# r of two batches by one transfer each, unused tables out, and new order tables, in an RWKV attention and MLP-mixer kernel

## The chip, the cores and the metric

The kernel runs on one core of a Trainium2 chip. A core has five instruction queues that run side by side: TensorE (PE, matrix products, with its weight loads shown apart as PEld), VectorE (DVE), ScalarE (ACT), GpSimd (POOL) and SyncE (SP, which here only issues transfers). Transfers run on 16 DMA engines; those that SP issues go through a hardware queue (q1 in the profile), those that POOL issues through a software queue (q0), which can convert f32 to bf16 on the way. The metric is the device time of one execution in microseconds (us), lower is better. A profile is taken of one execution and records when each instruction and each DMA packet ran.

## What is computed

The reference has two parts. The first is a linear attention with decay for 4 batches, 8 heads, 768 steps and a head size of 48:

```python
for t in range(S):
    kt, vt, rt = (k[:, :, t], v[:, :, t], r[:, :, t])
    cur = np.einsum('bhd,bhe->bhde', u[None] * kt, vt)
    y[:, :, t] = np.einsum('bhd,bhde->bhe', rt, state + cur)
    state = w[None, :, :, None] * state + np.einsum('bhd,bhe->bhde', kt, vt)
```

Its result, turned to x of 768 steps by 384 columns a batch, goes through an MLP mixer:

```python
xt = x.transpose(0, 2, 1)
h = np.maximum(xt @ w_tok1, 0.0) @ w_tok2
u = x + h.transpose(0, 2, 1)
h2 = np.maximum(u @ w_ch1, 0.0) @ w_ch2
return (u + h2).astype(np.float32)
```

w_tok1 is 768 by 256, w_tok2 256 by 768, w_ch1 384 by 1536 and w_ch2 1536 by 384. All inputs and the output are f32.

## The kernel before

**Chunks.** The 768 steps of a batch are 6 chunks of 128 steps. In a chunk the recurrence becomes matrix products: k and r are multiplied by tables of powers of the decay w (`wnat` for k; `wp`, or `wpair`, for r), rounded to bf16 (`kr`), and turned so that the head dimension lies on the partitions (`trk`, `tr_ps`, copied to `rka`, `rkb`). The scores (`at_ps`) are their products, a mask makes `AT` of them, and `y_ps` sums AT times v and r times the state `S` of the chunk before. The state itself (`kv_ps`) grows by k times v. The step's own term with u is a small sum (`pr`, `ad_ps`, `adg`) times v (`own`, written to `ydb` or `yd`). The sum goes to `x_b` in bf16.

**The loads.** k and v come per chunk: a tile of 128 partitions (steps) with 8 runs of 48 floats, 192 bytes each, 192 KB. For batches 0 and 1 (`wide`), r comes per window of two chunks: a partition holds two steps, the runs are 384 bytes, and a load `win` is 384 KB (lines 506 to 538); three buffers `win` take turns. For batches 2 and 3, r comes per chunk (`rt`). SP issues all of these. `HOLD` makes a load wait until another has landed, so about three loads of batch 0 are under way at a time; `GATES` makes a load wait for a weight.

**The weights.** POOL issues seven weight transfers, `w0` to `w6` (lines 540 to 563): w_tok1, w_tok2, the first third of w_ch1 (columns 0 to 511), the rest of w_ch1, and three parts of w_ch2. `W_DEP` says which load of k or v must have landed before each goes out. POOL is in order, so a weight also waits for the products that stand ahead of it there.

**The mixer.** For each batch: `hid` (x_b by w_tok1 into `h1_ps`, 12 products of 384 columns in one to three parts), `relu` into `h1r`, `back` (by w_tok2; for batch 0 added to turned x_b, `turn_x`, into `hx_ps` and copied to `uT`), 24 tasks `up` of 3 products (`z_ps`, by w_ch1), 24 `relu` into `zr`, and `down` (`h_ps`, by w_ch2), then `osb` and a store. Products `up` with index 0 to 3 need only w2, the others w3.

**The order.** The kernel does not run its loops as written. Each piece of work is a task with dependencies (`add`, `flex`); `Plan.run` (line 245) emits all of them in the order of the list `ORDER`, written out at the top. `ENGINES` says which of two engines does a task that either could do, `BUFS` which buffer of a pool each tile takes. Each engine then runs its instructions in just this order, and each waits for its semaphores. So `ORDER`, `BUFS`, `ENGINES`, `W_DEP`, `HOLD` and `GATES` set all queues. All instructions that the tasks emit carry one line, 294, of a helper, so the profile's groups are told apart by their tiles.

Around the change the queues of before stand like this (chunk numbers of batch 0 unless said; k0 is k of chunk 0). SP: r of window 0, r of window 1, k0, k1, r of window 2, v1, k3, k2, k4, v0, v2, v3, v4, k5, v5, then for batch 1: r of window 0, k0, v0, r of window 1, k2, v1, v2, k1, r of window 2. POOL, after tables and products: w0, `own` of chunks 0 and 2, a product of k5, w1, `own` of 3 and 4, w2, w3, and then products of batch 1. w0 waits for v2, w1 and w2 for k5, w3 for v3.

At the start PE runs 12 products of zeros (`NWARM`, `warm`), and `FILL` puts a few more in front of single tasks. `pairs` (lines 654 to 798), the table `wnpair`, `mask2`, `place` and some pools belong to a way of working on two chunks at a time that is switched off (`PAIRED = []`); the tables are still built.

Of the kernel before, what the change touches and what calls it, by code (L numbers as in the profile page):

```python
# [67 lines left out]
    0, 1, 2, 0, 1, 0, 2, 1, 0, 2, 1, 0, 2, 1, 0, 1, 2, 0, 1, 2, 0, 1, 2, 0,  # L68
],
    'AT1': [  # L70
    0, 1, 2, 0, 1, 0, 2, 1, 0, 2, 1, 0, 2, 0, 1, 2, 0, 1, 2, 0, 1, 2, 0, 1,
# [11 lines left out]
    0, 1, 2, 3, 4, 1, 0, 2, 3, 4, 1, 0, 2, 3, 1, 4, 0, 2, 3, 4, 1, 0, 2, 3,  # L83
],
    'adg2': [],
# [4 lines left out]
    0, 1, 2, 3, 4, 5, 0, 1, 4, 2, 3, 0, 4, 5, 1, 2, 3, 0, 5, 4, 1, 2, 3, 0, 5, 2, 1, 0, 3, 4,  # L90
],
    'krw': [],
    'kt': [
    0, 1, 2, 3, 4, 5, 0, 1, 2, 3, 4, 5, 0, 1, 2, 3, 4, 5, 0, 1, 2, 3, 5, 4,
],
    'ku': [
    0, 1, 2, 0, 0, 0, 2, 0, 1, 2, 1, 2,
# [13 lines left out]
],  # L111
    'osb': [
    0, 1, 2, 0, 1, 2, 2, 2, 1, 0, 0, 1, 2, 0, 1, 2, 0, 1, 2, 0, 1, 2, 0, 1, 2,
],
    'pr': [
    0, 1, 1, 0, 1, 0, 1, 0, 1, 0, 1, 1,
],
    'pr2': [],
    'rk': [
    0, 1, 2, 3, 0, 1, 3, 2, 0, 1, 2, 3,  # L120
],
    'rka': [
    0, 1, 2, 0, 1, 2, 0, 1, 2, 0, 1, 2,
],
    'rka2': [],
# [4 lines left out]
    0, 1, 0, 1, 0, 1, 0, 1, 0, 1, 0, 1,  # L130
# [4 lines left out]
    'rwin': [],  # L135
    'uT': [
    0, 1, 2, 3, 1, 0, 3, 2,
],
    'u_sb': [
    0, 1, 2, 0, 1,  # L140
],
    'vb': [
    0, 1, 2, 3, 4, 0, 1, 3, 2, 4, 0, 1, 2, 3, 0, 3, 4, 1, 3, 1, 2, 0, 4, 3,
],
    'vb2': [],
    'vt': [
    0, 1, 2, 3, 4, 5, 0, 1, 3, 2, 4, 5, 0, 1, 3, 2, 4, 5, 0, 1, 3, 2, 4, 5,
],
    'win': [
    0, 1, 2, 1, 0, 2,  # L150
],
    'yd': [
    0, 1, 2, 0, 1, 2, 0, 1, 2, 0, 1, 0, 2, 1, 0, 1, 2, 0,
],
    'ydb': [
    0, 1, 0, 1, 0, 1,
],
    'zr': [
    0, 1, 2, 1, 0, 1, 2, 0,
# [1065 lines left out]
```

## Time and profile before

| What | us |
|---|---|
| three runs | 165.94, 165.34, 166.04 |
| their median | 165.94 |
| span of the profiled execution, first to last instruction | 160.1 |
| PE busy | 153.4 |
| PE weight loads (beside PE) | 102.6 |
| DVE busy | 111.6 |
| POOL busy | 88.8 |
| ACT busy | 68.2 |

The time of the profiled execution as a whole is not listed beside its span; the median of the runs is 5.8 us above the span. In the lines of a timeline the columns are start in us, duration in us, engine, line, operation, tiles written and read with their shapes, count, and in brackets the idle time of the engine just before with what ended it. "SPq" and "POOLq" are the sequencers that issue transfers. PE's matmuls are pipelined, so the mean duration of one is longer than the distance between two.

### The profile page before, as it was taken

To read this page: it belongs to the slowest core of one execution; us is meant where nothing else is said; L and a number is where in the kernel's file an instruction comes from. 1 tells how busy PE (TensorE), PEld (TensorE's weight loads), DVE (VectorE), ACT (ScalarE), POOL (GpSimd) and SP (SyncE) were. 2 spreads that over 40 slices of the span, in tenths; PEclk is the share of its full clock that TensorE was granted. 3 is DMA by queue.
4 is the path that set the end of the run, shared out by engine and by line. 5 is a ranking of instruction groups with operands and counts; after the bars stand their busy time and mean duration, and the time that the engine had idled before them with its cause. 6 is when DMAs were issued, how large, how long until landed. Compare 5 with 4: busy or idle time off the path is not lost.

```text
span 160.1 us, 3797 instructions
## 1 busy us (share of the span) xinstructions
PE 153.4 (96%) x1463; PEld 102.6 (64%) x1463; DVE 111.6 (70%) x237; ACT 68.2 (43%) x150; POOL 88.8 (55%) x112
## 2 busy tenths in 40 slices
PE   6998799899999999999999999999999999999992
PEld 1464577567677677666767666677676556676572
DVE  6689884875697578397969939788997357422432
ACT  3999875438924254254524431144214102355000
POOL 7149991028179999899982997999822000000000
DMA  5999999999999979999999999999791064300222
GB/s 130 208 208 182 147 236 220 207 230 212 186 203 204 196 164 186 220 215 150 246 205 207 213 211 161 197 232 205 120 265 57 0 158 161 74 6 0 98 98 98
DMA packets 93061, 26.89 MB, mean 168 GB/s; under 512 B 87794, under 2 KB 92148, under 8 KB 93044
## 3 DMA queue, kind: packets, MB, share of 16 engines
q1 hardware_dynamic: 90688, 23.40, 72.6%
q0 software_dynamic: 2160, 3.15, 11.5%
q8 instruction: 11, 0.18, 0.5%
q10 hardware_dynamic: 196, 0.11, 0.2%
q14 instruction: 6, 0.05, 0.1%
HBM read 20.46 MB, written 4.72 MB: 157 GB/s over the span
## 4 chain that ended last, share of the span: by engine, by line
PE 76%; DMA 17%; ACT 2%; POOL 1%; issue 1%; SPq 1%; DVE 0%; POOLq 0%
PE h_ps L294 34%; PE z_ps L294 27%; DMA wch<-in_moe_w_ch_dram 7%; DMA kt<-in_k_dram 5%; DMA vt<-in_v_dram 5%; PE y_ps L294 4%; PE at_ps L294 3%; PE hT_ps L294 3%; PE kv_ps L294 2%; PE hx_ps L294 1%; PE trk L294 1%; ACT vb L294 1%; SPq L294 1%; PE tr_ps L294 1%; ACT x_b L294 1%
## 5 line engine op out<-in xcount | busy, mean ns | idle before, releaser
L294 PE MATMUL h_ps<-wch,zr 128*128 128x384 bf16 (+1 forms) x300 | 53.9, 320 | 0.0
L294 PE MATMUL z_ps<-uT,wch 128*128 128x384 bf16 x288 | 52.5, 327 | 0.6 <-DMA wch<-in_moe_w_ch_dram 0.6
L294 ACT ACTIVATE zr<-z_ps 128x384 bf16<-128x384 f32 x56 | 27.1, 492 | 39.5 <-PE z_ps L294 39.3
L294 PEld LDWEIGHTS <-wch 128*128 128x128 bf16 x288 | 31.1, 115 | 13.4 <-DMA wch<-in_moe_w_ch_dram 1.2
L294 PEld LDWEIGHTS <-zr 128*128 128x128 bf16 x300 | 27.6, 98 | 15.3
L294 DVE TENSOR_TENSOR AT<-at_ps,mask 128x512 bf16<-128x512 f32 x48 | 31.0, 683 | 3.7 <-PE at_ps L294 3.6
L294 DVE TENSOR_SCALAR zr<-z_ps 128x384 bf16<-128x384 f32 x40 | 21.4, 554 | 11.4 <-PE z_ps L294 8.6
L294 POOL TENSOR_TENSOR yd<-vb,adg 128x384 f32<-128x384 bf16 x18 | 14.8, 828 | 11.6 <-ACT vb L294 4.3
L294 POOL TENSOR_TENSOR kr<-kt,wnat 128x384 bf16<-128x384 f32 x19 | 19.3, 1019 | 3.0 <-DMA kt<-in_k_dram 2.9
L294 ACT CAST vb<-vt 128x384 bf16<-128x384 f32 x22 | 11.0, 511 | 12.6 <-DMA vt<-in_v_dram 12.6
L294 DVE TENSOR_TENSOR osb<-u_sb,h_ps 128x384 f32<-128x384 bf16 (+1 forms) x16 | 8.4, 528 | 9.9 <-PE h_ps L294 9.4
L294 PEld LDWEIGHTS <-kr 128*128 128x128 bf16 x176 | 11.8, 102 | 4.9 <-POOL kr L294 1.5
L294 POOL TENSOR_TENSOR ku<-kt,u_bc 128x384 f32<-128x384 f32 x12 | 12.1, 1008 | 0.5 <-DMA kt<-in_k_dram 0.5
L294 POOL TENSOR_TENSOR rku<-ku,rt 128x384 f32<-128x384 f32 x12 | 11.9, 1001 | 0.2
L294 POOL TENSOR_TENSOR kr<-rt,wp 128x384 bf16<-128x384 f32 x12 | 12.0, 1000 | 0.0
L294 PEld LDWEIGHTS <-wtok 128*128 128x128 bf16 x78 | 7.4, 98 | 4.4
L294 DVE TENSOR_TENSOR x_b<-y_ps,yd 128x384 bf16<-128x384 f32 x18 | 9.6, 549 | 0.6 <-PE y_ps L294 0.5
L294 PE MATMUL h_ps<-x_b,wtok 128*128 128x384 bf16 x48 | 8.8, 327 | 0.0
L294 PE MATMUL y_ps<-vb,AT 128*128 128x48 bf16 x192 | 8.7, 184 | 0.0
L294 ACT CAST S<-kv_ps 48x192 bf16<-48x192 f32 x18 | 5.6, 311 | 7.3 <-PE kv_ps L294 4.2
L294 POOL TENSOR_TENSOR pr<-rka,rkb 128x512 bf16<-128x512 bf16 x2 | 2.3, 1149 | 10.7 <-DVE rka L294 10.7
L294 DVE TENSOR_TENSOR u_sb<-x_b,hT_ps 128x384 bf16<-128x384 bf16 x15 | 7.6, 548 | 0.6 <-PE hT_ps L294 0.6
(93 smaller groups left out, 183.1 us busy)
## 6 DMA issues: line engine op xcount, KB each, us to landing
kt<-in_k_dram SPq DMA_DIRECT2D x24, 192.0 KB, 4.2
vt<-in_v_dram SPq DMA_DIRECT2D x24, 192.0 KB, 4.8
out_dram<-osb SPq DMA_DIRECT2D x23, 192.0 KB, 1.9
win<-in_r_dram SPq DMA_DIRECT2D x6, 384.0 KB, 4.9
rt<-in_r_dram SPq DMA_DIRECT2D x12, 192.0 KB, 3.2
wch<-in_moe_w_ch_dram POOLq DMA_DIRECT2D x4, 384.0 KB, 6.6
wtok<-in_moe_w_tok_dram POOLq DMA_DIRECT2D x2, 384.0 KB, 6.4
wch<-in_moe_w_ch_dram POOLq DMA_DIRECT2D x1, 768.0 KB, 11.3
```

Source lines behind the costliest of these rows:

```text
L294: return lambda *args, **kw: tc.keep_in_program_order(f(*args, **kw))
```

## The change

The diff, cut to its core; the lists `ORDER`, `BUFS` and `ENGINES` are replaced as a whole.

```diff
-W_DEP = [(0, 2, 2), (0, 5, 0), (0, 5, 0), (0, 3, 2), (1, 2, 0), (1, 1, 2), (1, 5, 0)]
-HOLD = {(0, 4, 1): (0, 2, 1),
...
-GATES = {(2, 0, 2): 1, (2, 4, 1): 3, (3, 1, 0): 2, (3, 1, 1): 6, (3, 5, 2): 5}
-NWARM = 12
...
-FILL = {138: 2, 154: 1, 159: 1, 190: 1}
+W_DEP = [(0, 0, 2), (0, 4, 2), (0, 5, 2), (0, 5, 2), (1, 1, 0), (1, 2, 0), (1, 1, 2)]
+HOLD = {(0, 2, 0): (0, 1, 0),
+        (0, 0, 2): (0, 0, 0),
+        (0, 1, 2): (0, 3, 0),
+        (0, 2, 2): (0, 2, 0),
+        (0, 4, 0): (0, 0, 2),
+        (0, 5, 0): (0, 1, 2),
+        (0, 3, 2): (0, 2, 2),
+        (0, 4, 2): (0, 4, 0),
+        (0, 5, 2): (0, 5, 0),
+        (1, 0, 1): (0, 3, 2),
+        (1, 0, 0): (0, 4, 2)}
+GATES = {(1, 0, 0): 2}
+NWARM = 17
...
+FILL = {130: 3, 171: 1, 185: 2}
...
-    t_wn2 = [decay(wn2, j, j, [t_io2]) for j in range(2)]
...
     def load(b, c, i):
         nm, src = (("kt", k), ("rt", r), ("vt", v))[i]
-        win = two_steps(b, c, i)
-        nm = "win" if win else nm
+        whole = i == 1 and wide(b)
 
         def f():
-            if win:
-                t = sb("win", [128, H, 2 * D], f32)
-                dst = t
-                what = src[b, :, ds(c * T, 2 * T), :].rearrange("h (p j) d -> p h (j d)", j=2)
+            if whole:
+                t = sb("rw", [128, H * NWIN, 2 * D], f32)
+                got = sp.dma_start(t, src[b].rearrange("h (w p j) d -> p (h w) (j d)", p=T, j=2))
+                for cc in range(C):
+                    asked[b, cc, i] = got
+                    loaded[b, cc, i] = t.rearrange("p (h w) e -> p h w e", w=NWIN)[:, :, cc // 2, :]
             else:
...
```

A key is (batch, chunk, input), with input 0 for k, 1 for r and 2 for v. One buffer `rw` of 1152 KB takes the place of the three `win`; the r of batch 1 goes into the same buffer, so it waits until all r products of batch 0 have read it. `mask2`, `place`, `wnpair` and `pairs` go. The Exp tables that only batches 2 and 3 use (`wnat` for groups of three chunks, `wp`) and their state tables are mostly built later.

The built program of the changed kernel has these queues. SP: r of batch 0, k1, k0, k3, k2, v0, v1, v2, k4, k5, v3, v4, v5, then r of batch 1, k0, k1, k2, k3, v0, v1, k5, k4 of batch 1. POOL: products of r and k, the u product, the mask, w0, a `pr`, a table, `own` of 0 and 1, a product of k4, `own` of 2, a `pr`, `own` of 3, w1, w2, w3, then two products of batch 1's r. `own` of chunks 4 and 5 is on DVE. On DVE, the two products of r for window 1 of batch 1 stand after the copy of the last x_b of batch 0 and ahead of the second `relu` into `h1r`; on PE their turn stands ahead of the first `back`, and the turn of window 0 ahead of the first `up`. Of the tasks that either engine could do, 64 `relu` into `zr` and `h1r` are on ACT and 40 on DVE (60 and 44 before).

More of the change, by code (lines that the diff above doesn't have):

```diff
@@ L67 @@
     'AT0': [
-    0, 1, 2, 0, 1, 0, 2, 1, 0, 2, 1, 0, 2, 1, 0, 1, 2, 0, 1, 2, 0, 1, 2, 0,
+    0, 1, 2, 1, 0, 2, 1, 0, 2, 1, 0, 2, 0, 1, 2, 0, 1, 0, 2, 0, 1, 2, 0, 1,
 ],
     'AT1': [
-    0, 1, 2, 0, 1, 0, 2, 1, 0, 2, 1, 0, 2, 0, 1, 2, 0, 1, 2, 0, 1, 2, 0, 1,
+    0, 1, 2, 1, 0, 2, 1, 0, 2, 1, 0, 2, 0, 1, 2, 1, 0, 2, 1, 2, 0, 1, 2, 0,
 ],
@@ L82 @@
     'adg': [
-    0, 1, 2, 3, 4, 1, 0, 2, 3, 4, 1, 0, 2, 3, 1, 4, 0, 2, 3, 4, 1, 0, 2, 3,
+    0, 1, 2, 3, 4, 0, 1, 2, 3, 4, 0, 2, 1, 4, 0, 3, 2, 4, 1, 0, 4, 3, 2, 0,
 ],
-    'adg2': [],
     'h1r': [
@@ L89 @@
     'kp': [
-    0, 1, 2, 3, 4, 5, 0, 1, 4, 2, 3, 0, 4, 5, 1, 2, 3, 0, 5, 4, 1, 2, 3, 0, 5, 2, 1, 0, 3, 4,
+    0, 1, 2, 3, 4, 5, 0, 2, 1, 4, 3, 2, 0, 5, 1, 4, 2, 0, 5, 3, 4, 2, 1, 0, 5, 3, 2, 4, 0, 1,
 ],
-    'krw': [],
     'kt': [
-    0, 1, 2, 3, 4, 5, 0, 1, 2, 3, 4, 5, 0, 1, 2, 3, 4, 5, 0, 1, 2, 3, 5, 4,
+    0, 1, 2, 3, 4, 5, 0, 1, 2, 3, 5, 4, 0, 1, 3, 2, 5, 4, 0, 1, 3, 2, 5, 4,
 ],
     'ku': [
-    0, 1, 2, 0, 0, 0, 2, 0, 1, 2, 1, 2,
+    0, 1, 2, 0, 1, 2, 0, 1, 2, 0, 1, 0,
 ],
@@ L102 @@
     'm': [
[8 rows of a table removed]
[7 rows of a table added]
 ],
     'osb': [
-    0, 1, 2, 0, 1, 2, 2, 2, 1, 0, 0, 1, 2, 0, 1, 2, 0, 1, 2, 0, 1, 2, 0, 1, 2,
+    0, 1, 2, 0, 1, 0, 0, 2, 2, 2, 0, 0, 0, 2, 2, 0, 1, 2, 2, 1, 2, 0, 1, 2, 0,
 ],
     'pr': [
-    0, 1, 1, 0, 1, 0, 1, 0, 1, 0, 1, 1,
+    0, 1, 0, 1, 0, 1, 1, 0, 1, 0, 1, 0,
 ],
-    'pr2': [],
     'rk': [
-    0, 1, 2, 3, 0, 1, 3, 2, 0, 1, 2, 3,
+    0, 1, 2, 3, 0, 1, 2, 3, 1, 0, 2, 3,
 ],
     'rka': [
-    0, 1, 2, 0, 1, 2, 0, 1, 2, 0, 1, 2,
+    0, 1, 2, 0, 1, 2, 0, 2, 1, 0, 2, 0,
 ],
-    'rka2': [],
     'rkb': [
@@ L129 @@
     'rku': [
-    0, 1, 0, 1, 0, 1, 0, 1, 0, 1, 0, 1,
+    0, 1, 1, 0, 1, 0, 1, 0, 0, 1, 0, 1,
 ],
@@ L134 @@
 ],
-    'rwin': [],
+    'rw': [
+    0, 0,
+],
     'uT': [
@@ L139 @@
     'u_sb': [
-    0, 1, 2, 0, 1,
+    0, 1, 2, 0, 2,
 ],
     'vb': [
-    0, 1, 2, 3, 4, 0, 1, 3, 2, 4, 0, 1, 2, 3, 0, 3, 4, 1, 3, 1, 2, 0, 4, 3,
+    0, 1, 2, 3, 4, 0, 1, 2, 3, 4, 0, 2, 1, 3, 0, 1, 4, 3, 0, 2, 1, 3, 4, 2,
 ],
-    'vb2': [],
     'vt': [
[L147 to L150, printed above, removed]
+    0, 1, 2, 3, 4, 5, 0, 1, 2, 3, 4, 5, 0, 1, 3, 4, 0, 2, 1, 5, 3, 4, 0, 2,
 ],
     'yd': [
-    0, 1, 2, 0, 1, 2, 0, 1, 2, 0, 1, 0, 2, 1, 0, 1, 2, 0,
+    0, 1, 2, 0, 1, 2, 2, 1, 0, 1, 2, 2, 0, 2, 1, 0, 2, 0,
 ],
@@ L158 @@
     'zr': [
-    0, 1, 2, 1, 0, 1, 2, 0,
+    0, 1, 2, 0, 1, 0, 2, 1,
 ],
@@ L162 @@
 ENGINES = [
[9 rows of a table removed]
-]
-W_DEP = [(0, 2, 2), (0, 5, 0), (0, 5, 0), (0, 3, 2), (1, 2, 0), (1, 1, 2), (1, 5, 0)]
-HOLD = {(0, 4, 1): (0, 2, 1),
-        (0, 1, 2): (0, 0, 0),
-        (0, 3, 0): (0, 1, 0),
-        (0, 2, 0): (0, 4, 1),
-        (0, 4, 0): (0, 1, 2),
-        (0, 0, 2): (0, 3, 0),
-        (0, 2, 2): (0, 2, 0),
-        (0, 3, 2): (0, 4, 0),
-        (0, 4, 2): (0, 0, 2),
-        (0, 5, 0): (0, 2, 2),
-        (0, 5, 2): (0, 3, 2),
-        (1, 0, 1): (0, 4, 2),
-        (1, 0, 0): (0, 5, 0)}
-GATES = {(2, 0, 2): 1, (2, 4, 1): 3, (3, 1, 0): 2, (3, 1, 1): 6, (3, 5, 2): 5}
-NWARM = 12
-WIDE_AT = [
-    0, 1, 2, 3, 4, 5, 6, 7, 8, 9, 10, 11,
-]
-FILL = {138: 2, 154: 1, 159: 1, 190: 1}
[9 rows of a table added]
+]
+W_DEP = [(0, 0, 2), (0, 4, 2), (0, 5, 2), (0, 5, 2), (1, 1, 0), (1, 2, 0), (1, 1, 2)]
+HOLD = {(0, 2, 0): (0, 1, 0),
+        (0, 0, 2): (0, 0, 0),
+        (0, 1, 2): (0, 3, 0),
+        (0, 2, 2): (0, 2, 0),
+        (0, 4, 0): (0, 0, 2),
[7 more added lines that the diff above has]
+NWARM = 17
+WIDE_AT = [0, 1, 2, 3, 4, 5, 6, 7, 8, 9, 10, 11, 12, 13, 14, 15, 16]
+FILL = {130: 3, 171: 1, 185: 2}
 POOL_ONLY = [
@@ L195 @@
 ]
-PAIRED = []
 GB = [
@@ L209 @@
  ('dma', 'dve'), ('dma', 'dve'), ('dma', 'dve'), ('dma', 'dve')]
-NKRW = 2
 PE_ADDS = [
@@ L340 @@
     warm = const.tile([128, 512], bf16, name="warm")
-    NW = C // 2
+    NWIN = C // 2
     iota_i = const.tile([128, 4 + 2 + 2 * NG], i32, name="iota_i")
@@ L346 @@
     mask = const.tile([128, 128], f32, name="mask")
-    mask2 = const.tile([128, 2, 128], f32, name="mask2")
-    place = const.tile([128, 2, 128], bf16, name="place")
     lnw = const.tile([128, dm], f32, name="lnw")
@@ L357 @@
     wp2 = const.tile([128, 2, dm], f32, name="wpair")
-    wn2 = const.tile([128, 2, dm], f32, name="wnpair")
     u_blk = const.tile([128, HP, H], bf16, name="u_blk")
@@ L389, in iotas_pair @@
     def iotas_pair():
-        iota_of(0, [[-1, 2]], T - 1, -2)
         iota_of(2, [[1, 2]], -T, 2)
@@ L398 @@
     t_iop = once("POOL", "iotas2", iotas_pair)
-    t_io2 = once("DVE", "cast_io", lambda: dve.tensor_copy(iota[:, 0:4], iota_i[:, 0:4]), [t_iop])
+    t_io2 = once("DVE", "cast_io", lambda: dve.tensor_copy(iota[:, 2:4], iota_i[:, 2:4]), [t_iop])
     t_ioi = once("POOL", "iotas", iotas)
@@ L411 @@
     t_mask = once("POOL", "mask", make_mask)
-    def make_mask2():
-        pool.memset(mask2, 1.0)
-        for q in range(2):
-            rows = mask2[q * P:(q + 1) * P]
-            pool.affine_select(out=rows, in_=rows, compare_op=ALU.is_gt, fill=0.0, base=0, pattern=[[-1, 2], [1, 128]],
-                               channel_multiplier=-2)
-    t_mask2 = once("POOL", "mask2", make_mask2)
-    def make_place():
-        dve.memset(place, 0.0)
-        for q in range(2):
-            rows = slice(q * P, (q + 1) * P)
-            for j in range(2):
-                dve.tensor_copy(place[rows, j, j::2], ident[rows, rows])
-    t_place = once("DVE", "place", make_place, [t_id])
     ZERO = {"DVE": "memset_pad", "POOL": "memset_padp"}
@@ L504, in wide @@
         return STYLE[b * C][0] == "f32"
-    def two_steps(b, c, i):
-        return (b, c // 2) in PAIRED or (i == 1 and wide(b))
     def load(b, c, i):
         nm, src = (("kt", k), ("rt", r), ("vt", v))[i]
-        win = two_steps(b, c, i)
-        nm = "win" if win else nm
+        whole = i == 1 and wide(b)
         def f():
-            if win:
-                t = sb("win", [128, H, 2 * D], f32)
-                dst = t
-                what = src[b, :, ds(c * T, 2 * T), :].rearrange("h (p j) d -> p h (j d)", j=2)
-            else:
-                t = sb(nm, [128, dm], f32)
-                dst = h3(t)
-                what = src[b, :, ts(c, T), :].rearrange("h s d -> s h d")
-            asked[b, c, i] = sp.dma_start(dst, what)
-            loaded[b, c, i] = t
+            if whole:
[4 more added lines that the diff above has]
+                    loaded[b, cc, i] = t.rearrange("p (h w) e -> p h w e", w=NWIN)[:, :, cc // 2, :]
+            else:
+                t = loaded[b, c, i] = sb(nm, [128, dm], f32)
+                got = asked[b, c, i] = sp.dma_start(h3(t), src[b, :, ts(c, T), :].rearrange("h s d -> s h d"))
             if (b, c, i) in GATES:
-                after(asked[b, c, i], sent[GATES[b, c, i]])
+                after(got, sent[GATES[b, c, i]])
             if (b, c, i) in HOLD:
-                after(asked[b, c, i], asked[HOLD[b, c, i]])
-        return add("SP", "load2" if win else "load", f, [], take=(nm,))
+                after(got, asked[HOLD[b, c, i]])
+        return add("SP", "loadw" if whole else "load", f, [], take=("rw" if whole else nm,))
     for b in range(B):
@@ L534 @@
             for i in range(3):
-                if c % 2 and two_steps(b, c, i):
-                    t_load[b, c, i] = t_load[b, c - 1, i]
+                if c and i == 1 and wide(b):
+                    t_load[b, c, i] = t_load[b, 0, i]
                 else:
@@ L596, in evac_r @@
                  W["tr"].rearrange("p j a s -> p a s j"))
-        m0 = flex(PRODUCT, mul_r(0), [lr, t_wp2[0]] + t_kp0, take=("kp",), use=[(lr, "win")])
-        m1 = flex(PRODUCT, mul_r(1), [lr, t_wp2[1], m0], use=[(lr, "win"), (m0, "kp")])
+        m0 = flex(PRODUCT, mul_r(0), [lr, t_wp2[0]] + t_kp0, take=("kp",), use=[(lr, "rw")])
+        m1 = flex(PRODUCT, mul_r(1), [lr, t_wp2[1], m0], use=[(lr, "rw"), (m0, "kp")])
         t_tr = add("PE", "tr_all", turn_r, [m0, m1, t_id], take=("m",), use=[(m0, "kp")])
@@ L1172 @@
         for cs in GROUPS[b]:
-            if (b, cs[0] // 2) not in PAIRED:
-                units(b, cs)
-            elif cs[0] % 2 == 0:
-                pairs(b, cs[0] // 2)
+            units(b, cs)
         mixer(b)
```

125 lines of the change are left out of this document (removed), and 115 rows, old and new, of tables (BUFS, ENGINES, ORDER).

## Prediction

> **What bounds the kernel now.** I read the page's head first, then the chain of waits in order of time, then TensorE's own waits in the stretch that the chain gives to it.
>
> ```profile
> span 160.1 us, 3797 instructions
> PE 153.4 (96%) x1463; PEld 102.6 (64%) x1463; DVE 111.6 (70%) x237; ACT 68.2 (43%) x150; POOL 88.8 (55%) x112
> ```
>
> PE is busy for 96% of the span; no other engine is near that. The chain of waits says which part of it counts (columns: start, us, what):
>
> ```profile
> 1.94 5.11 DMA kt<-in_k_dram
> ...
> 7.12 3.64 DMA vt<-in_v_dram
> ...
> 10.78 3.04 DMA kt<-in_k_dram
> ...
> 13.84 4.03 DMA vt<-in_v_dram
> ...
> 22.25 0.83 POOL ydb L294
> 23.08 0.75 POOL wch L294
> 23.83 11.26 DMA wch<-in_moe_w_ch_dram
> 35.09 0.05 issue
> 35.14 2.14 PE z_ps L294 x12
> ...
> 148.06 9.14 PE h_ps L294 x68
> 157.21 0.02 issue
> 157.23 0.35 DVE osb L294
> ```
>
> It has two halves. Up to 35.09 us it is transfers: loads of batch 0 that follow each other by HOLD, some small work, and then the issue of the second part of w_ch1 (w3), which lands 11.26 us later. From 35.14 to 157.21 us it is PE alone. How dense PE is there, the waits in 35.2 to 157 us tell (total, times, longest):
>
> ```profile
> PEld L294 <- issue: 2.1, 7, 0.3
> ```
>
> So in 122 us there are 2.1 us that a better order could win, and the tail after 157.21 us (2.9 us) is one half-width sum and its store, in both kernels. The time is decided by when PE becomes dense. That start is set by the transfers:
>
> ```profile
> DMA packets 22307, 6.88 MB, mean 196 GB/s; under 512 B 20637, under 2 KB 21791, under 8 KB 22303
> ...
> DMA packets 8539, 1.63 MB, mean 181 GB/s; under 512 B 8538, under 2 KB 8538, under 8 KB 8538
> ...
> q1 hardware_dynamic: 8538, 1.62, 96.8%
> ...
> DMA packets 2064, 0.77 MB, mean 258 GB/s; under 512 B 2063, under 2 KB 2064, under 8 KB 2064
> ```
>
> These are the DMA view's answers for 0 to 35.1, 9 to 18 (k and v, 192-byte runs) and 2 to 5 us (r, 384-byte runs). The 16 engines are covered 96.8% of the time while k and v come.
>
> **The change, part by part.** The sum is made against the span, 160.1 us; the runs' median is 165.94 us, so 5.8 us lie around it, which I keep.
>
> *One transfer for r.* The runs stay 384 bytes and their number stays 3072 per batch, so the bytes cost what they cost. What moves is the first use:
>
> ```profile
> 0.81 1.08 SPq L294 DMA_DIRECT2D win<-in_r_dram  x2
> 6.00 0.37 SPq L294 DMA_DIRECT2D win<-in_r_dram  x1
> 6.08 1.96 DVE L294 TENSOR_TENSOR kr<-win,wpair 128x384 bf16<-128x384 f32 x4 [1.35 <-DMA win<-in_r_dram]
> ```
>
> The third r load is held until the second has landed: 6.0 us, and the first products start at 6.08. With all of r in front, 0.39 MB more must come, 1.5 us at 258 GB/s: they start at 7.5 us. This costs nothing at the end, because the k and v loads behind set the pace; the warm-up matmuls, now 17, fill that time.
>
> The Trainium skill, page "DMA: Bandwidth & Descriptors", section "Anatomy of one DMA", gives each transfer about 2.0 us of fixed cost, and its section "Bandwidth" asks for 1 MiB a transfer; four transfers fewer would be 8 us by that figure, an estimate. The 96.8% above does not agree: three loads are under way at a time, and the fixed part of one is hidden under the others.
>
> *Tables.* Gone are two Exp tables, a mask and a placing matrix; most of the eight tables that only batches 2 and 3 need move out of the first 17 us to later.
>
> ```profile
> 5.41 0.60 ACT L294 ACTIVATE wnpair<-lnw,iota 128x384 f32<-128x384 f32 x1
> 8.44 0.60 ACT L294 ACTIVATE wnpair<-lnw,iota 128x384 f32<-128x384 f32 x1
> 1.55 0.87 POOL L294 TENSOR_SCALAR_AFFINE_SELECT mask<-mask 64x256 f32<-64x256 f32 x2
> 3.80 0.65 DVE L294 COPY place<-ident 64x64 bf16<-64x64 bf16 x4
> ```
>
> 1.2 us of ACT, some 1.2 of POOL and 0.8 of DVE go. All of it stood in the wait for r, k and v, so I count 0; uncovered it would be 1.2 us, once. The tables built later fall on an ACT that is 43% busy.
>
> *Where the weights and batch 1's r now stand.* This decides. The rows of before:
>
> ```profile
> 16.81 1.02 POOL L294 DMA_DIRECT2D wtok<-in_moe_w_tok_dram  x1
> 20.62 0.60 POOL L294 DMA_DIRECT2D wtok<-in_moe_w_tok_dram  x1
> 23.02 1.66 POOL L294 DMA_DIRECT2D wch<-in_moe_w_ch_dram  x2
> ...
> 19.63 0.51 ACT L294 CAST vb<-vt 128x384 bf16<-128x384 f32 x1
> 20.41 0.65 ACT L294 CAST S<-kv_ps 48x192 bf16<-48x192 f32 x2
> ...
> DMA to landing us min/median/max: 6.2/6.4/6.5
> ```
>
> (the last row is wtok's). After: r lands at 7.5; the three loads behind it at 8.6, 9.6 and 10.7 (1.06 us each, 181 GB/s). Then come three chains of three hops, 3.3 us a hop (three loads of 0.197 MB at 181 GB/s; the rows have 3.04 to 4.03). The first of w_tok1, w0, waits only for v of chunk 0 (12.9 us), so it goes out near 13.5 instead of 16.81, and pushes the last loads back by its own 2.7 us (0.39 MB at the 146 GB/s below). v of chunks 3, 4, 5 lands near 21.1, 22.2, 23.2.
>
> ```profile
> DMA packets 577, 0.29 MB, mean 146 GB/s; under 512 B 12, under 2 KB 577, under 8 KB 577
> ```
>
> (19 to 21 us, w0 of before.) Batch 1's whole r (1.18 MB) goes out at 21.1, behind v of chunk 5, and takes 22.3 to 26.9 us at 258 GB/s, landing about 27.4. w1 waits for v of chunk 4 and stands on POOL behind the product `own` of chunk 3, which waits for v of that chunk and, on ACT, for the cast (0.51) and a state copy (0.65): 21.1 + 1.16 + 0.83 (the ydb row of the chain) = 23.1 us instead of 20.62. w2 follows at 23.7, w3 at 24.5 instead of 23.83.
>
> PE's rows in this stretch:
>
> ```profile
> 26.57 0.49 PE L294 MATMUL h_ps<-x_b,wtok 128*128 128x384 bf16 x2
> 27.64 2.11 PE L294 MATMUL hx_ps<-wtok,h1r 128*128 128x384 bf16 x12
> 29.59 0.61 PE L294 MATMUL tr_ps<-ident,kr 128*128 128x128 bf16 x8
> 30.65 3.12 PE L294 MATMUL z_ps<-uT,wch 128*128 128x384 bf16 x18 [0.46 <-DMA wch<-in_moe_w_ch_dram]
> 33.61 0.39 PE L294 MATMUL trk<-ident,kr 128*128 128x128 bf16 x4
> ```
>
> In the new order DVE does two r products of batch 1 (0.55 us each) before the second `relu` of h1, and PE turns them before the first `back`: behind that wait stand `back`, the copies of uT and every `up`. With r at 27.4 these cost 1.1 us, and `back` can start at 29.0; but w_tok2 lands only at 23.1 + 6.2 = 29.3 (before, 20.62 + 6.2 = 26.8). So `back` runs from 29.3 to 31.4 (2.11), a turn takes 0.61, and the first `up` stands at 32.0 instead of 30.65. Eight `up`s need only the first part of w_ch1: 24 matmuls, of which 18 took from 30.65 to 33.61, so 3.9 us: 35.9 us.
>
> w3's landing, bounded from both sides: its own issue plus the row, 24.5 + 11.26 = 35.8; and by bytes, batch 0 (3.54 MB), r of batch 1 (1.18), w_tok (0.79) and w_ch1 (1.18) make 6.69 MB against 6.88, 1.0 us less at 196 GB/s, so 34.1. Batch 1's k now waits until w2 has landed, which keeps it out. I take 35.7 for both, nearer to the issue row, since POOL's place is what that row shows. PE is dense 0.55 us later, with a second turn of r done by then (0.61) and the turn of k of chunk 0 still to do (0.39): 0.22 us less is left.
>
> *From there on* the work is the same 122 us. The new tables can win at most the 2.1 us above and can lose more; I take 0.
>
> Sum: 160.1 + 0.55 - 0.22 = 160.4 us, a run of 166.3 us. The landing reaches from -1.0 (bytes) to +0.8 (the eight `up`s), so the forecast's own range, less the far end of the bytes and with 0.5 us for the later stretch, is 165.1 to 167.4.
>
> **Rivals.**
>
> *r of batch 1 is caught behind the weights (slower).* In 30 to 33 us both queues had work:
>
> ```profile
> q0 software_dynamic: 264, 0.53, 93.6%
> q1 hardware_dynamic: 252, 0.09, 17.8%
> ```
>
> So q1 gets 84 packets a us beside the weights, against 688 alone (2064 in 3 us, above). It decides where w_tok2's first packet comes, between its issue at 23.1 and r's end at 26.9 us. If it comes 0.4 us before that end, 275 packets remain, 3.3 us of them: r lands at 30.3, DVE holds the relu of h1 until 31.4 + 0.5, and `back` and every `up` behind it start 2.8 us after 29.3: 169.1. A whole us would cost 8. For it: w1 is issued 3.8 us before r's end. Against: w_tok's transfers took over 6 us from issue to landing, with little before them in their own queue. The Trainium skill, "DMA: Bandwidth & Descriptors", section "Queues, rings and completion order", says that each DMA engine takes turns between the queues packet by packet; by that rule the 264 against 252 is expected, and the trace agrees.
>
> *The rest of the tables meets new waits (slower).* Batch 1's k and v all start after w2 and run into wch2's two transfers; the cast of v of chunk 1 stands on DVE in front of relus that free PE's banks. 1.5 us there: 167.8.
>
> *The loads come as the bytes say, and some of the 2.1 us goes (faster).* 160.1 - 1.0 - 0.22 - 0.5: 158.4, a run of 164.2. For it: w0 no longer runs alone (146 GB/s). Against: w1 is issued later.
>
> *Fewer transfers save their gaps (faster).* The mechanism of the fixed cost; at most the 3.2% that 9 to 18 us leaves open, 1.0 us of 33: 165.0.
>
> **How the numbers follow.** Forecast 0.35, caught r 0.18, new waits 0.16, bytes 0.27, gaps 0.04. A measurement of this kernel can tell about 0.5% (0.83 us) from no change. Of the forecast 0.02 is faster, 0.23 the same and 0.10 slower; bytes give 0.24 and 0.03, gaps 0.02 and 0.02, new waits 0.02 same and 0.14 slower, caught r 0.18 slower. Faster 0.28, same 0.30, slower 0.42. The range 163.8 to 170.0 leaves out the worse half of caught r and the best of bytes.
>
> **What would show it.** First r products near 7.5 us; `hid` of the last chunk near 27; batch 1's r landed by 27.5; first `up` near 32; a wait of PE for wch that ends at 35 to 36.5, and none over 0.5 us after. I am wrong if PE stands over 1 us at the turn of batch 1's r, if w3 lands before 34.5, or if PE's waits after 36 us exceed 3 us.

## The result and the profile after

| Kernel | median of its runs, us | ratio to before, 95% interval |
|---|---|---|
| before (four runs) | 165.64 | |
| changed (four runs: 170.88, 170.76, 170.43, 169.08) | 170.59 | 1.0289 (1.0211 to 1.0367) |

The change costs 5.0 us. The forecast was 166.3, and the time lies 0.6 us above the upper end of its range. A run more than 1.5% above the fastest one of its kernel is left out of the ratios, but not of the medians of the experiments below.

The profiled execution of the changed kernel took 170.88 us. From its page:

```profile
span 169.2 us, 3774 instructions
PE 158.6 (94%) x1469; PEld 105.0 (62%) x1469; DVE 111.9 (66%) x223; ACT 67.7 (40%) x158; POOL 89.1 (53%) x109
PEclk9995579999999999999999999999999999999999
```

TensorE is 5.2 us longer busy than before with six more instructions: some of its work ran slower. The last row (granted clock by fortieth of the span, 4.2 us each) says where: in the fourth and fifth slice, 12.7 to 21.2 us, the clock stood at half. The chain of waits up to the first `up` (start, us, what):

```profile
0.87 7.47 DMA rw<-in_r_dram
...
8.44 2.68 DVE kr L277 x3
11.12 0.34 issue
11.45 3.03 DVE kr L277 x2
14.48 0.05 issue
14.53 0.61 PE trk L277 x4
...
20.36 1.82 PE at_ps L277 x11
...
24.42 0.61 ACT wnat L277
...
32.96 0.98 DVE ydb L277
...
36.55 2.12 PE hx_ps L277 x15
38.67 0.45 PE tr_ps L277 x8
39.12 0.97 PE z_ps L277 x6
```

Before, this chain was k, v and weight transfers up to 35.09 us. Now one transfer stands on it, r, and behind its landing at 8.34 us everything is computation in order: five products on DVE, TensorE's turns and scores, ACT's copies and casts. No k, v or weight stands on it. The first `up` stands at 39.12 us instead of 30.65. Three views show what happens in it. The first groups the early products (ns min/median/max, first and last start):

```profile
L277 DVE TENSOR_TENSOR kr<-rw,wpair x4: 558/1343/1349, 8.4 to 11.5; 128x384 bf16<-128x384 f32 x4
L277 POOL TENSOR_TENSOR kr<-rw,wpair x2: 1304/1336/1367, 8.5 to 11.1; 128x384 bf16<-128x384 f32 x2
```

Since all of r lands at once, DVE and POOL begin together, and a product that takes 0.55 us alone takes 1.34 on DVE and as long on POOL. Two engines did two products in 1.34 us that DVE alone does in 1.1. The second view gives TensorE by stretch (length, busy time, products, granted clock, DMA share, GB/s), the third POOL's queue around the issues of w1, w2 and w3:

```profile
10.00:12.80 2.80, 0.30 (x4) 1.00 0.78 152
12.80:15.00 2.20, 0.87 (x9) 0.59 1.03 188
15.00:23.00 8.00, 8.00 (x60) 0.50 1.07 173
```

```profile
29.59 0.83 POOL L277 TENSOR_TENSOR ydb<-vb,adg 128x384 bf16<-128x384 bf16 x1
30.36 0.60 POOL L277 DMA_DIRECT2D wtok<-in_moe_w_tok_dram  x1
30.96 1.52 POOL L277 DMA_DIRECT2D wch<-in_moe_w_ch_dram  x2
```

TensorE stood idle for 2.5 of 2.8 us, its clock fell, and it then worked without a pause for 8.0 us at half speed. From 15 to 23 us TensorE thus set the pace itself, at half speed. `own` of chunk 3 came at 29.59, late behind this, and w1 to w3 behind it at 30.36 to 31.7.

Behind the first `up` little more is lost. PEld's waits from 39.2 to 167 us (total, times, longest):

```profile
PEld L277 <- issue: 1.5, 5, 0.3
PEld L277 <- DMA uT<-u_sb: 1.0, 2, 0.8
PEld L277 <- DVE kr L277: 0.3, 1, 0.3
PEld L277 <- ACT vb L277: 0.3, 1, 0.3
```

That is 3.1 us where the kernel before had 2.1. From its first `up` to its end the changed kernel takes 130.1 us (169.2 less 39.12), the kernel before 129.5 (160.1 less 30.65). So nearly all of the loss was made by 39 us.

### The profile page after: what moved, and what is told of

Its sections match the earlier page's. It is cut to its first block, busy times and chain, and to the rows that moved or that the text cites. A ratio compares the mean times of both kernels' runs of the same rounds, so it can differ in the third digit from the quotient of the medians.

```text
span 169.2 us, 3774 instructions
## 1 busy us (share of the span) xinstructions
PE 158.6 (94%) x1469; PEld 105.0 (62%) x1469; DVE 111.9 (66%) x223; ACT 67.7 (40%) x158; POOL 89.1 (53%) x109
## 4 chain that ended last, share of the span: by engine, by line
PE 81%; DMA 7%; DVE 4%; ACT 4%; issue 1%; SPq 0%; DVEq 0%; ACTq 0%
PE h_ps L277 33%; PE z_ps L277 25%; DMA rw<-in_r_dram 4%; PE at_ps L277 4%; PE y_ps L277 4%; DVE kr L277 3%; PE kv_ps L277 3%; DMA uT<-u_sb 3%; PE hT_ps L277 3%; PE hx_ps L277 3%; PE trk L277 2%; PE tr_ps L277 2%; ACT S L277 1%; PE ad_ps L277 1%; ACT rkb L277 1%
## 5 line engine op out<-in xcount | busy, mean ns | idle before, releaser
L277 PE MATMUL z_ps<-uT,wch 128*128 128x384 bf16 x288 | 51.7, 326 | 0.5 <-DMA uT<-u_sb 0.5
L277 PEld LDWEIGHTS <-wch 128*128 128x128 bf16 x288 | 31.7, 114 | 13.9 <-DMA uT<-u_sb 1.0
L277 DVE TENSOR_SCALAR zr<-z_ps 128x384 bf16<-128x384 f32 x37 | 19.5, 551 | 13.3 <-PE z_ps L277 13.2
L277 PEld LDWEIGHTS <-kr 128*128 128x128 bf16 x176 | 12.6, 106 | 8.6 <-DVE kr L277 4.5
L277 ACT CAST vb<-vt 128x384 bf16<-128x384 f32 x23 | 11.6, 515 | 4.2 <-DMA vt<-in_v_dram 4.2
L277 PE MATMUL kv_ps<-warm 128*128 128x512 bf16 (+1 forms) x19 | 8.7, 599 | 2.2 <-DVE warm L277 1.7
L277 DVE TENSOR_TENSOR kr<-rw,wpair 128x384 bf16<-128x384 f32 x8 | 6.5, 848 | 4.8 <-DMA rw<-in_r_dram 4.8
L277 ACT COPY rkb<-tr_ps 128x1024 bf16<-128x1024 bf16 x4 | 4.0, 1012 | 13.0 <-PE tr_ps L277 13.0
```

The source lines that it names most:

```text
L277: return lambda *args, **kw: tc.keep_in_program_order(f(*args, **kw))
```

## The experiments

**What is a usual execution of before?** The kernel before, unchanged.

> The kernel before, unchanged, to see the span of a usual execution of it. In the changed kernel the run lies 1.7 us above the span (170.88 against 169.2); of the kernel before only one span is known, 160.1, and a run of 165.6. If about 1.7 us lie around the span in both, the usual span of before is near 164 and the change costs about 5 us in the span too; if 5.8 us lie around it in before, the span is near 160 and the change costs 9 us in the span, of which 4 are given back outside it. I expect a span of 163 to 164.5 and a run of 164.5 to 166.

Ten runs, 164.03 to 169.14 us; each lies 1.6 to 1.8 us above its span (164.03 with 162.3, 166.30 with 164.6). So 1.7 us lie around the span in both kernels, and the execution whose profile the prediction read, span 160.1, was quicker than any of these. The usual span of before is near 163.5; the change costs about 5 us there too.

**Are the slow products a matter of the two engines?**

```diff
 ENGINES (products of r: window 0 first half, window 1 second half; of k: chunks 1 and 2)
-0, 0, 0, 0    # POOL
+1, 1, 1, 1    # DVE
```

> The changed kernel with the four early products of k and r that POOL does (r of window 0 and of window 1, k of chunks 1 and 2) given to DVE; the order of the list stays, so DVE now has ten products in a row. Theory 'turns': a product on DVE takes 1.34 us while POOL is in one of its own and 0.55 alone; then each takes 0.5 to 0.6 us here, the last half of window 0 is done at 11.6 instead of 12.7 and the last product near 14, the first turn of r ends 1.2 us earlier, k of chunk 0 two us earlier, and the run is 168 to 169.5. Rival 'layout': the products are slow because they read r out of the large buffer; then they stay at 0.9 to 1.3 us on DVE, ten of them reach to 19 us and the run is 172 to 175.

169.19 us, ratio 1.0215 (1.0097 to 1.0333). The early products in this run:

```profile
L277 DVE TENSOR_TENSOR kr<-rw,wpair x6: 544/550/636, 8.5 to 12.1; 128x384 bf16<-128x384 f32 x6
L277 DVE TENSOR_TENSOR kr<-kt,wnat x4: 532/546/805, 10.4 to 13.4; 128x384 bf16<-128x384 f32 x4
```

The same products out of the same buffer take 0.55 us with POOL out of the way, so "layout" is out and "turns" is shown for the products. In the time it is worth 1.4 us by the medians (170.59 to 169.19); the intervals of this kernel and the changed one overlap.

**Is it the order of the products?** As e2, and in `ORDER`:

```diff
-118, 190, 154, 191, 138, 119, 122, 155, 174    # window 0, 2, 1, 2, k1, window 0, k0, window 1, k3
+118, 119, 138, 122, 154, 155, 174, 190, 191    # window 0, k1, k0, window 1, k3, window 2
```

> As the run before, and the ten products in another order: both of window 0 first, then k of chunks 1 and 0, window 1, k of chunk 3, window 2. Theory 'start': the time is lost because the first turn of r stands at 12.85 (7.18 in the kernel before) and TensorE sits idle until 14.5 and then runs at half its clock until 23. Here the turn stands near 9.6, the idle time is gone, the half clock too, and the first up comes 3 to 5 us earlier than 39.1: a run of 165.5 to 167.5. Rival 'later chain': what decides stands behind 20 us (the casts and copies in ACT's order, the place of the second weight behind own of chunk 3); then the start is won and lost again, and the run is above 169.

168.62 us, ratio 1.0204 (1.0110 to 1.0299): between the two theories. The turn came at 9.3 as expected, but TensorE then idled for 1.2 and 0.7 us ahead of the turns of k of chunks 0 and 3, and its clock was still at 0.51 from 12.7 to 19.5.

**Is it the clock?** Two kernels with more products of zeros (`warm`): e4 is the changed kernel with twelve ahead of the first turn, e5 is e3 with nine.

```diff
-NWARM = 17
+NWARM = 29    # e4: twelve ahead of the first tr_all
+NWARM = 26    # e5: six ahead of the turn of k of chunk 0, three ahead of that of chunk 3
```

> The changed kernel with twelve more products of zeros on TensorE ahead of the first turn of r, to cover its idle time from 9.9 to 12.85; nothing else is changed. Theory 'clock': the half clock between 13.4 and 23.2 costs time on the path; here the granted clock stays at 1.0, the turns, scores and fills of that stretch take half as long, and the run is 167 to 169. Rival: DVE and ACT set that stretch and TensorE only waits for them; then the clock is full and the run is within 0.5 us of 170.6.

> The kernel of the run e3_window0_first with nine more products of zeros on TensorE, six between the first turn of r and the turn of k of chunk 0, three ahead of the turn of k of chunk 3: the two places where TensorE sat idle there (9.9 to 11.2 and 12.0 to 12.7). In that run the clock still fell, from 13.0 to about 19, and from 12.7 to 20.2 TensorE was never idle, so there the half clock does set the pace. Theory 'clock': with it kept, that stretch takes 2 to 3.5 us less, the first up comes at 33 to 34 instead of 35.8, and the run is 165.5 to 167 against 168.6. Rival: the waits for DVE and ACT behind it take the gain back, as in the run with more warm-up alone; run 168 to 169.

e4: 171.0 us, 1.0343 (1.0231 to 1.0454). The first wait was covered but the next ones (2.4 us with 0.81 busy from 12.6) were not; the clock fell two us later, to 0.57 from 15 to 19. Its first `up` came 1.9 us earlier, and TensorE then waited 1.9 us, ahead of scores of batch 1, for a `relu` into `zr` on DVE. e5: 168.37 us, 1.0216 (1.0129 to 1.0304), the same as e3. So the half clock is real, but neither run shows that keeping it full wins time. They could not show it well: e4 moved the fall, and in e9 and e10 below, which have the same cover as e5, the clock was full up to 19 us and fell later, to 0.50 from 23 to 25 us in e9 and from 21 to 27 in e10. None of these kernels kept it through the stretch, so "clock" is neither shown nor excluded.

**Is it the number of transfers in batch 0?** e6 is e5 with r of batch 0 read by three transfers issued one behind the other.

```diff
-got = sp.dma_start(t, src[b].rearrange(...))
+got = [sp.dma_start(t[window w], src[b, :, ds(2 * w * T, 2 * T), :].rearrange(...)) for w in range(NWIN)]
```

> As the run before, but r of batch 0 comes by three transfers, one a window, into the same buffer, and DVE takes windows 0 and 1 of r first, then k of chunks 1, 0 and 3, then window 2. This undoes the one transfer for batch 0 alone. If the one transfer is what makes the start late, the products of r are done before k lands, k of chunk 3 is multiplied near 11.6 instead of 12.5, and the run is 0.7 to 1.5 us faster than the run before. If k and v set the pace, as the prediction had it, it is within 0.5 us of it.

169.09 us, 1.0203 (1.0102 to 1.0303): no gain. So in the changed kernel's order, three transfers in a row ahead of k are no better than one. The chain of waits of this kernel shows what it met instead:

```profile
14.01 7.63 DMA kt<-in_k_dram
21.64 0.02 issue
```

k of chunk 5 was 7.6 us under way, beside w0, issued at 13.3 (in e3 the same load took 5.9 us, in the changed kernel 4.7). In e9 (w0 held until k of chunk 5 has landed: `W_DEP[0] = (0, 5, 0)`, and w0 behind `pr` of chunk 1 on POOL) and e10 (the same from e5):

> The kernel of e6_r_in_three (three r transfers, products of window 0 first and on DVE, more warm-up) with w0, the first weight, held until k of chunk 5 has landed instead of v of chunk 0, and so moved on POOL behind the product pr of chunk 1. In e6 and e5 TensorE then waited for k of chunk 5: issued at 14.0 and 14.8, landed 7.6 and 6.5 us later, beside w0, which was issued 0.7 us ahead of it; the other loads of k take 2.8 to 4 us. Theory 'stacked limits': with the products and the clock mended, the early w0 is the next limit. Then k of chunk 5 lands near 17, the wait of 2.9 us at 20.4 goes, and the run is 165 to 167 against 169.1. Rival: w0 only pushes the same time further on (v of chunks 4 and 5, the hidden layer's first part, or batch 1's r): 168 to 169.5.

> The same with r of batch 0 by one transfer (the kernel of e5_window0_first_warm with w0 later). If the one transfer for batch 0 has no price of its own once products, clock and w0 are mended, it is within 0.8 us of e9_three_r_w0_later; if it has one, it is 1 us or more slower than that.

```profile
14.33 3.08 DMA kt<-in_k_dram
17.40 0.30 issue
...
17.82 0.93 issue
18.75 0.99 POOL wGm L279
19.74 1.22 POOL ydb L279 x2
```

In e9's chain the same load takes 3.1 us, but POOL now stood waiting in front of w0, and the state table and two `own` behind it came late: 168.94 us, 1.0203 (1.0110 to 1.0295). The rival of e9 held: the time is pushed on. e10 took 171.01 us, its runs from 168.98 to 175.53, too scattered to set beside e9; its two shortest, 168.98 and 169.67, lie among those of e9 (167.56 to 170.52), so a price of the one transfer in this order is not shown.

**Which part of the change is it?** Now from the other side: the kernel before, with one part of the change. e7 has r of both batches by one transfer, all else as before; e8 leaves out the two tables `wnpair`, `mask2` and `place`.

```diff
+                if c:
+                    return
+                t = sb("rw", [128, H * NW, 2 * D], f32)
+                got = sp.dma_start(t, src[b].rearrange("h (w p j) d -> p (h w) (j d)", p=T, j=2))
...
-t_mask2 = once("POOL", "mask2", make_mask2)
+t_mask2 = once("POOL", "mask2", lambda: None)
```

> The kernel before, with its own order, buffers and tables, and r of batches 0 and 1 by one transfer each at the place of the first window's load (one buffer of three windows in place of three buffers). Prediction's step: the first products move from 6.1 to about 8, and nothing comes of it at the end, since k and v set the pace: a run within 0.8 us of the kernel before. Theory now: the first products at 8.4 instead of 6.1, TensorE idle for two us, the clock down from about 11 for some 8 us: 2 to 4 us slower, 167 to 169. If it is 3 us or more slower by itself, the one transfer is most of the loss; if under 1, the loss is in the new order.

> The kernel before without the work that nothing reads: the two Exp tables wnpair, mask2 and place are not made. All else stays. The prediction counts 0 for this, since it stands in the wait for the loads: within 0.5 us of the kernel before. Rival: it stood on DVE, ACT or POOL ahead of the first products and its 1.2 us come off: 164.

e7: 169.66 us, ratio 1.0298 (1.0220 to 1.0375), as much as the whole change. e8: 164.50 us, 0.9970 (0.9921 to 1.0019), no difference that can be told. So in the order of before the one transfer alone costs as much as the whole change, and the unused tables nothing. That this is also what the changed kernel loses does not follow: there e6 took it back for batch 0 and gained nothing. e11 and e15 put twelve `warm` into e7, e11 on both sides of the first turn, e15 all ahead of it:

> The kernel of e7_before_with_one_r (169.7) with twelve more products of zeros on TensorE, four ahead of the first turn of r and eight ahead of the second, to cover the 1.8 us waits there. In that run the clock was at half from 10.2 to 20.6, and TensorE's work of that stretch stood ahead of the tables on ACT and POOL behind which w0 was issued at 20.4 (16.8 before). Theory 'clock': with the clock kept, TensorE is through that stretch 2 to 3 us earlier, w0 goes out near 17.5, ahead of batch 1's r, and the run is 166 to 167.5. Rival 'late r alone': the clock is a side effect and the run stays at 169 to 170.

> The kernel of e7_before_with_one_r with twelve more products of zeros, all ahead of the first turn of r, so that TensorE is busy from 7.4 until the fourth product of r is done near 11. Theory 'clock': the clock stays full, the stretch that took from 11.3 to 20.4 there is 2 to 3.5 us shorter, w0 is issued near 17.5 and the run is 166 to 168. Rival: the lateness alone costs it, and the run stays at 169 to 170.

e11: 169.83 us, 1.0253 (1.0164 to 1.0343); its cover stood behind the wait and ran at half clock itself. e15: 168.28 us, its runs 166.49, 166.79, 169.78 and 170.10; a wait of 1.1 us was left and the clock fell again, 0.50 from 13.5 to 19. The two shorter runs lie about 2 us under the shortest of e7 (168.71), the two longer ones do not, and no ratio can be given. Neither kernel kept the clock, so the clock's own share in e7 stays open.

**Which batch?** One kernel of before with the common buffer, `rw`, and a switch:

```diff
+ONE = (0,)    # e12; (1,) in e13, () in e14: the batches whose r comes by one transfer
...
+                if b in ONE:
+                    got = sp.dma_start(R[b] as a whole, src[b].rearrange(...))
+                else:
+                    got = sp.dma_start(R[b][:, :, c // 2, :], src[b, :, ds(c * T, 2 * T), :].rearrange(...))
```

> The kernel before with r of batch 0 by one transfer into the common buffer, and r of batch 1 by three transfers into slices of that buffer, each at its old place. Theory (a): the start decides, 168 to 170, with the half clock from 10 to 20 as in e7_before_with_one_r. Theory (b): within 1 us of the kernel before, 164.5 to 166.

> The kernel before with r of batch 0 by three transfers at their old places and r of batch 1 by one, at the place of its first window. Theory (a): within 1 us of the kernel before. Theory (b): w0 or w1 lands 3 to 4 us later than in before, the hidden layer's first part or back waits for it, 167.5 to 169.5.

> Control: the kernel before with the common buffer and its strided slices, but all six transfers of r as before. If neither the buffer nor the layout of the slices costs, it is within 0.8 us of the kernel before; a product of r takes 0.5 to 0.6 us on DVE when POOL is not in one. If it is 2 us or more slower, the buffer is the cause in place of the transfer.

| Kernel | r by one transfer in | median, us | ratio to before |
|---|---|---|---|
| e14 | no batch | 163.90 | 0.9976 (0.9937 to 1.0015) |
| e12 | batch 0 | 167.92 | 1.0230 (1.0166 to 1.0293) |
| e13 | batch 1 | 167.42 | 1.0227 (1.0155 to 1.0300) |
| e7 | both | 169.66 | 1.0298 (1.0220 to 1.0375) |

The buffer and its slices cost nothing; each batch's one transfer costs 3.5 to 4 us by itself by the medians, and the two together less than their sum, for a reason that is not shown. The two lose at different places. In e12 the first `up` stands at 36.2 us (31.4 in e14), and behind it the two kernels take the same 130 to 131 us. In e13 it stands at 32.8, and 134.3 us follow. Batch 0: the timelines of DVE and TensorE, first e14, then e12.

```profile
6.11 1.96 DVE L295 TENSOR_TENSOR kr<-rw,wpair 128x384 bf16<-128x384 f32 x4 [1.36 <-DMA rw<-in_r_dram]
...
7.19 1.33 PE L295 MATMUL tr_ps<-ident,kr 128*128 128x128 bf16 x16
8.95 0.78 PE L295 MATMUL trk<-ident,kr 128*128 128x128 bf16 x8 [0.42 <-DVE kr L295]
9.65 0.91 PE L295 MATMUL u_ps<-wp,ones 1*128 1x384 f32 x2
```

```profile
8.21 3.17 DVE L295 TENSOR_TENSOR kr<-rw,wpair 128x384 bf16<-128x384 f32 x4 [3.46 <-DMA rw<-in_r_dram]
...
8.82 0.61 PE L295 MATMUL tr_ps<-ident,kr 128*128 128x128 bf16 x4 [1.43 <-DVE kr L295]
10.97 1.46 PE L295 MATMUL tr_ps<-ident,kr 128*128 128x128 bf16 x12 [1.54 <-DVE kr L295]
12.22 1.06 PE L295 MATMUL trk<-ident,kr 128*128 128x128 bf16 x8
13.21 1.64 PE L295 MATMUL u_ps<-wp,ones 1*128 1x384 f32 x2
```

The products start 2.1 us later, take 1.2 us longer beside POOL, TensorE waits 3.0 us in two pieces, and its next rows are longer (1.06 against 0.78, 1.64 against 0.91). By 13.2 us it is 3.6 us behind. The pages, first e14's, then e12's, show what the rest of the loss is:

```profile
PE 153.7 (95%) x1462; PEld 102.3 (63%) x1463; DVE 111.3 (69%) x237; ACT 68.4 (42%) x150; POOL 88.9 (55%) x112
```

```profile
PE 158.2 (95%) x1462; PEld 105.1 (63%) x1463; DVE 112.4 (68%) x237; ACT 68.5 (41%) x150; POOL 88.3 (53%) x112
```

The same 1462 products take TensorE 4.5 us longer, and its time outside them is 8.5 us of the span of 162.2 in e14 and 8.0 of 166.2 in e12. So e12 does not idle more in all: its late start uses up the pauses that e14 has later, and what it loses appears as slower products. What it would take at full clock was not measured. Batch 1: the waits of TensorE in e13, then the landing of w1 there and in e14 (us from issue, one transfer).

```profile
PE trk L295 <- DVE kr L295: 2.3, 2, 2.0
PE hx_ps L295 <- DMA wtok<-in_moe_w_tok_dram: 2.2, 1, 2.2
```

```profile
DMA to landing us min/median/max: 9.3/9.3/9.3
```

```profile
DMA to landing us min/median/max: 5.9/5.9/5.9
```

Batch 1's r, issued at 19.2, took 11.3 us to land, and w1, issued beside it at 21.0, 9.3 instead of 5.9: `back` waited 2.2 us for it, where e14 has a wait of 1.2 us of the first `up` for w2. Then k of batch 1, behind r in its queue, came late and cost another 2.0, and behind that wait the clock was at 0.50 from 39 to 42 us: 18 products of `up` took 4.77 us there, against 3.12 for the 18 ahead of the wait. TensorE did not wait between them, so 1.6 us of this execution, 168.86 us, is the half clock itself; the three other runs, 167.31 to 167.51, are shorter by about as much.

**And in the changed kernel?** e17 has batch 1's r by three transfers at the place of the one; e16 has batch 0's loads as before has them, with the ten early products on DVE and the first turn of r ahead of the last products of zeros:

```diff
 e16, on top of e3
+get(0); got = get(1)                              # r of windows 0 and 1, then k1 and k0
+after(last_window.pop()(2), asked[0, 2, 1])       # r of window 2 behind k0, when window 1 has landed
-W_DEP = [(0, 0, 2), ...
+W_DEP = [(0, 5, 0), ...                           # and w0 behind the state table on POOL
```

> The changed kernel with batch 0's start as before has it: r by three transfers, the third held until the second has landed and issued behind k of chunks 1 and 0; w0 held until k of chunk 5 has landed and moved on POOL behind the state table; the ten early products on DVE, windows 0 and 1 first; the first turn of r ahead of the last four products of zeros. Batch 1's r stays whole, the late tables stay late. Theory: batch 0's late start is most of the 5 us in the changed kernel too; the first turn stands near 8, the first up near 32.5 to 34 and the run at 165.5 to 167.5. Rival: the changed kernel's own order (ACT's row of casts, own of chunk 3 ahead of the second weight) costs as much by itself; 168 to 169.5.

> The changed kernel with batch 1's r by three transfers at the place of the one, all else unchanged. In the changed kernel the whole r was issued at 21.8 and had landed at 29.0, before w1 was issued at 30.4, so it stood beside no weight. Expected: within 0.8 us of the changed kernel, 170 to 171.3. If it is 2 us or more faster, batch 1's whole transfer costs here as it does in the kernel before.

e17: 169.81 us, 1.0232 (1.0171 to 1.0294); it cannot be told from the changed kernel. So batch 1's one transfer has no price here that can be seen. e16: 168.36 us, 1.0153 (1.0088 to 1.0218), about half of the loss back, not all, and inside the range of its rival. But e3, on which it builds, stood at 1.0204 already, and the two intervals overlap: what batch 0's loads alone give back is not settled. Its first `up` is at 36.0; one place where it loses, DVE's row first, then POOL's:

```profile
28.82 2.17 DVE L279 TENSOR_TENSOR ydb<-vb,adg 128x384 bf16<-128x384 bf16 x1 [0.58 <-ACT adg L279]
```

```profile
28.61 1.96 POOL L279 TENSOR_TENSOR kr<-rw,wpair 128x384 bf16<-128x384 f32 x2
```

`own` of the last chunk, 0.56 us on DVE at 24.54 in the timeline of before, took 2.17 beside POOL's two products of batch 1's r, and TensorE waited 1.5 us for it. The rest is not taken apart: how the changed kernel's loss divides between the one transfer of batch 0 and the new order stays open.

**A version a little faster than before.** e18 is e14 without the unused tables.

> The kernel before with what was harmless or better in the runs so far: the unused tables gone (e8: ratio 0.997) and one buffer of three windows read by three transfers a batch (e14: 0.998). Expected: 0.3 to 1 us faster than the kernel before, 163.6 to 164.3 beside 164.5; if the two do not add up, within 0.3 us of it.

164.20 us, ratio 0.9892 (0.9831 to 0.9952): about 1% faster than the kernel before. Its median lies between those of e14 (163.90) and e8 (164.50), which could not be told from before, so more than a small gain should not be read into it. It keeps three transfers a batch, the order and the place of all other tables.

## Why the prediction was wrong, by its steps

**What bounds the kernel.** Right for before, and kept true for the changed kernel without reason: the chain there has no load behind r. The base was off as well: 5.8 us "around the span" are 1.7 us, since the profile was of an unusually quick execution. The difference that the forecast worked out is not touched by that.

**One transfer for r: the step that failed.** "This costs nothing at the end, because the k and v loads behind set the pace; the warm-up matmuls, now 17, fill that time." The first part was sized 7.5 us and measured 8.44, a small miss. The conclusion fell: no load of k or v stands on the changed kernel's chain behind r, and its first `up` came at 39.12 us. In the order of before, batch 0's part alone (e12) is 1.0230 (1.0166 to 1.0293), some 4 us. How much of the changed kernel's 5.0 us it makes stays open (e6, e10 and e16). Three things were not in the working. All ten products of r and k become ready at nearly the same time, on two engines that slow each other (1.34 us against 0.55, shown by e2). The warm-up ran out at 9.5, and TensorE idled up to 14.5 apart from one turn in two halves of 0.4 us; its granted clock was 0.50 from 13.4 to 23, and in e12 such slower products are as much as the whole loss. And computation had no slack behind the loads: from 14.5 to 39 us the chain is work in order, in which TensorE was idle for 0.9 us in all.

The products' rows agree in part with the Trainium skill, page "SBUF — State Buffer", section "SBUF: two separate sides": DVE and GpSimd share a port pair that one instruction holds as a whole while the other blocks. That the two delay each other is what the rows show (0.55 us alone, 1.34 together). Taking turns as a whole would make 1.55 us a pair, with the 1.00 us of such a product on POOL alone in e14, and the pairs took 1.34.

**Tables.** Right that they cost nothing: e8 is 0.9970 (0.9921 to 1.0019). The late table `wnat` stands on the chain at 24.42 with 0.61 us; that it costs this was not tried.

**Weights and batch 1's r.** The issues of w0 (13.5 told, 14.58 measured) and r (21.1, 21.76) were near, r's landing (27.4, 28.99) 1.6 us off. w1 to w3 were told for 23.1 to 24.5 and came at 30.36 to 31.70: the working let `own` of chunk 3 follow the landing of v, and it followed the late computation. So the first `up` was put 7.1 us too early, and the wait for w3 that the sum rests on (0.55 us later than before, w3 landed at 35.7) did not occur: w3, issued at 31.7, landed near 41.8, and no product stood waiting for it.

**The rivals.** "Caught r" named the right contention and was near in price (169.1), but its place was wrong. In the kernel before it is real: e13, where w1 is slowed beside r rather than r behind w_tok2. In the changed kernel r had landed 1.4 us before w1 went out. Beside w0, k of chunk 5 took 4.7 us there and nothing waited for it. "New waits" in the rest: told 1.5 us, measured 1.0 more than before in PEld's waits. "Bytes" and "gaps": no run was faster for fewer transfers. The 2.0 us a transfer that the prediction takes from the Trainium skill, page "DMA: Bandwidth & Descriptors", section "Anatomy of one DMA", are measured there on transfers that GpSimd issues, and r is issued by SP.

**What would show it.** Of the listed signs these failed: the first r products (7.5 told, 8.44), the landing of batch 1's r (27.5, 28.99), the first `up` (32, 39.12), `hid` of the last chunk (27, near 35), the wait for wch that was to end at 35 to 36.5 (there is none), and PEld's waits (3.1 us, over the 3 named). TensorE did not stand at the turn of batch 1's r, but in front of batch 0's.

## What to carry to other kernels

Where an input comes in parts, ask what starts on the first part: one transfer of the same bytes delays the first use to the last byte, makes all its users ready at once, and stands longer beside other queues. In the order of the kernel before this cost over 3 us in each of two batches; in the changed order no price of batch 1's could be seen. A load "sets the pace" only while the computation behind it is not later than the load, so work out both chains. Count what a wait does to TensorE's clock behind it, not only the wait. And take the base of a sum from the spans of several executions, not from one profile.

## What the hardware showed that was not expected

TensorE's clock fell after short waits and did not come back soon. In the changed kernel it fell near 13.2 us, when TensorE had worked for some 0.7 of the last 3.7 us, its longest wait 2.6; in e12, by the durations of its products, two waits of 1.4 and 1.5 us with 0.6 us of work between were enough. In the changed kernel TensorE was then busy for all of 15 to 23 us at 0.50. The Trainium skill, page "TensorE: Matmul & The Clock Gate", section "What's actually happening", has the clock released after about 3.4 us of activity; here it took 8.0 us, in e3 some 6.8, so the measurement differs.

A fall of the clock can also be missing from the records. In e12 the clock reads 1.00 for all of 10.9 to 20, and yet the products of zeros of 512 columns in it (ns min/median/max):

```profile
10.90:20.00 9.10, 9.03 (x67) 1.00 0.98 185
```

```profile
L295 PE MATMUL at_ps<-warm x4: 607/631/634, 14.8 to 21.5; 128*128 128x512 bf16 x4
```

In the profile of before the same products:

```profile
L294 PE MATMUL at_ps<-warm x4: 378/380/390, 10.5 to 15.3; 128*128 128x512 bf16 x4
```

In the changed kernel, where the clock is recorded at 0.50, they took 634. So the duration of a known product tells the clock more surely than the row of the clock.
